# Pairs of tiles of one expert by Strassen's seven products, in a mixture-of-experts kernel whose bound is TensorE

## The chip, the cores and the metric

The kernel runs on one core of a Trainium2 chip. The metric is the device time of one execution in microseconds (us). All arithmetic that matters here is float32. The engines are called TensorE (PE in the profile, its weight loads PEld), VectorE (DVE), ScalarE (ACT), GpSimd (POOL) and SyncE (SP). SBUF and PSUM are the two on-chip memories that hold the program's tiles (matmuls write to PSUM), and the large arrays lie in DRAM. A transfer (DMA) *lands* when the profile shows it complete. The *granted clock* is the share of full speed that the profile gives for TensorE.

## The reference, cut to what matters

A causal linear attention (not touched by the change) makes 3072 tokens of 512 values. Each token then goes to one of eight experts, and its expert is two dense layers:

```python
h = np.maximum(x[b, s] @ w1[e], 0.0)      # 512 -> 1024
out[b, s] = p[e] * (h @ w2[e])            # 1024 -> 512
```

The expert `e` follows from the token's logits and a second gate, so how many tokens each expert gets is known only while the kernel runs. The kernel sorts the tokens by expert into tiles of up to 128 tokens (a half tile holds up to 64): a gather fetches a tile's rows from DRAM, and a scatter writes the result rows to their places.

## The kernel before

Most of the time after the attention goes into tiles, one after the other, in this order.

```python
def hidden(g, half):                      # layer 1 of tile g, half of the 1024 columns
    # ... (for half 0: a new buffer hts[g])
    ph = pg.tile([P, FT // 2, P], F32, name=f"ps{half}")
    for i in range(FT // 2):
        f = FT // 2 * half + i
        for d in range(DT):
            nc.tensor.matmul(ph[:, i], lhsT=w1t[g % 2][:, d, P * f:P * f + P], rhs=xtt[g % 2][:, d],
                             start=(d == 0), stop=(d == DT - 1))
    nc.scalar.activation(hts[g][:, FT // 2 * half:FT // 2 * half + FT // 2], ph, ACT.Relu)

def output(g):                            # layer 2
    ht = hts.pop(g)
    for f in range(FT):
        nc.tensor.matmul(pys[g % 2], lhsT=ht[:, f], rhs=w2t[g % 2][:, f], start=(f == 0), stop=(f == FT - 1))

def written(g):                           # times the chance, then the scatter
    i, j = at(g)
    y = act.tile([P, DM], F32, name="y")
    nc.vector.tensor_scalar(y, pys[g % 2], gate[i][:, j:j + 1], None, ALU.mult)
    nc.gpsimd.indirect_dma_start(out=out, out_offset=bass.IndirectOffsetOnAxis(ap=sidx[i][:, j:j + 1], axis=0),
                                 in_=y, in_offset=None, bounds_check=N - 1, oob_is_err=False)
# ... in an arm of the program, for each tile:
ahead(g + 2)                              # gather of the tile after the next, GpSimd
hidden(g, 0)
hidden(g, 1)
turned(g + 1)                             # four transposes of the next tile, copied to SBUF
output(g)
written(g)
weights(g + 2)                            # 4 MB of weights, if the expert changes
```

Counts that depend on the data (how many half tiles, how many extra tiles) are handled by branches into arms, one arm for each count.

## Time and profile before

| | before |
|---|---|
| time, median of the runs beside the changed kernel | 493.98 us (492.26 to 494.51, 4 runs) |
| span of the profiled run | 493.0 us |
| TensorE busy | 475.2 us, 96% |
| mean granted TensorE clock | 0.991 |
| VectorE / GpSimd busy | 127.3 / 106.8 us |

This is GpSimd's timeline in the same stretch of the kernel before (start us, duration us, then engine, line, operation, what is written and read; in brackets how long the engine sat idle before it, and what ended that):

```profile
341.17 1.00 POOL L659 DMA_INDIRECT out_dram<-y,sidx  x1 [5.29 <-DVE y L658]
347.96 1.04 POOL L621 DMA_INDIRECT xg<-x_dram,gidx  x1 [5.79 <-PE po L636]
355.62 1.01 POOL L659 DMA_INDIRECT out_dram<-y,sidx  x1 [6.62 <-DVE y L658]
```

GpSimd only starts gathers and scatters here. Scatters are 14.45 us apart, one for each tile, and each waits for its data. The list of GpSimd's waits (us in total, times, longest) has, among others, this:

```profile
POOL out_dram L659 <- DVE y L658: 179.3, 21, 13.9
...
POOL out_dram L829 <- DMA out_dram<-y,sidx: 13.2, 2, 6.6
```

A scatter that follows another scatter soon (L829 is a half tile's, issued right behind a full tile's) waits until the earlier one has landed, up to 6.6 us. Both write the tensor `out`, and the built program puts a wait for the first one's landing before the second. Between full tiles this wait is over long before the data is ready, so it can't be seen.

### The profile page before, as it was taken

The numbers are of one execution on the slowest core, as the hardware profiler recorded it, in microseconds if no ns is written. First come the engines' busy times: TensorE is split into PE (matmuls) and PEld (weight loads), VectorE is DVE, ScalarE is ACT, GpSimd is POOL, SyncE is SP. The second block draws the span as 40 slices with busy tenths as digits, with TensorE's granted clock in tenths as the row PEclk, the third lists the DMA queues.
The fourth block names the chain that finished last, engine by engine and source line by source line (L and its number), as shares of the span: only waits on it lengthen the run. The fifth ranks groups of instructions, "written<-read, shape, count | busy, mean of one in ns | idle before, by whom it ended". The sixth has DMA issues, their size and how long they took to land. (4 is left out here: it accounts for less than half of the span.)

```text
span 493.0 us, 10193 instructions
## 1 busy us (share of the span) xinstructions
PE 475.2 (96%) x4231; PEld 351.6 (71%) x4231; DVE 127.3 (26%) x315; ACT 84.7 (17%) x212; POOL 106.8 (22%) x118
## 2 busy tenths in 40 slices
PE   6999999989999999999999999999999999999992
PEld 5877788776777667658657856876667777666770
DVE  6645677652367301011010101101110110110000
ACT  2256656331110000000000001000000000000000
POOL 5575564300101300221011100201101101110000
PEclk9899999999999999999999999999999999999997
DMA  7999999996788999999999997699954980894000
GB/s 272 411 418 380 352 342 330 401 368 233 260 319 292 324 378 399 395 376 397 398 333 386 398 398 277 211 330 319 327 194 157 310 314 31 284 332 169 23 25 17
DMA packets 49850, 146.42 MB, mean 297 GB/s; under 512 B 3244, under 2 KB 3244, under 8 KB 46960
## 3 DMA queue, kind: packets, MB, share of 16 engines
q1 hardware_dynamic: 42096, 125.86, 69.9%
q0 software_dynamic: 4224, 13.37, 7.1%
q10 hardware_dynamic: 3456, 6.29, 3.4%
q8 instruction: 36, 0.59, 0.5%
q14 instruction: 38, 0.31, 0.2%
HBM read 153.90 MB, written 12.98 MB: 338 GB/s over the span
## 5 line engine op out<-in xcount | busy, mean ns | idle before, releaser
L646 PEld LDWEIGHTS ps<-xt,w 128*128 128x128 f32 x1536 | 175.0, 192 | 14.0 <-issue 12.9
L646 PE MATMUL ps<-xt,w 128*128 128x128 f32 x1536 | 177.1, 276 | 0.8 <-DVE xt L631 0.8
L653 PE MATMUL pk<-w,ht 128*128 128x512 f32 x384 | 168.8, 592 | 0.0
L653 PEld LDWEIGHTS pk<-w,ht 128*128 128x128 f32 x384 | 71.1, 190 | 80.4 <-issue 80.4
L648 ACT ACTIVATE ht<-ps 128x512 f32<-128x512 f32 x48 | 28.7, 598 | 314.7 <-PE ps L646 314.2
L659 POOL DMA_INDIRECT out_dram<-y,sidx x24 | 24.6, 1026 | 196.3 <-DVE y L658 179.3
L658 DVE TENSOR_SCALAR y<-pk,gate 128x512 f32<-128x512 f32 x24 | 18.0, 751 | 146.0 <-PE pk L653 140.6
L637 DVE COPY xt<-po 128x512 f32<-128x512 f32 x23 | 15.9, 691 | 143.2 <-PE po L636 143.1
L621 POOL DMA_INDIRECT xg<-x_dram,gidx x24 | 25.0, 1041 | 121.2 <-PE po L636 84.1
L189 DVE TENSOR_TENSOR sm<-ps,mask 128x512 f32<-128x512 f32 x46 | 29.6, 685 | 15.1 <-PE ps L185 15.0
L165 POOL TENSOR_TENSOR qd<-inp,lamq 128x512 f32<-128x512 f32 x20 | 25.6, 1282 | 23.3 <-PE po L212 8.8
L185 PE MATMUL ps<-inp 64*64 64x128 f32 x736 | 26.3, 282 | 2.0 <-DMA inp<-in_qkv_dram 2.0
L225 PE MATMUL po<-sm,inp 128*64 128x128 f32 x384 | 26.9, 284 | 0.3 <-DMA inp<-in_qkv_dram 0.3
L225 PEld LDWEIGHTS po<-sm,inp 128*64 128x64 f32 x384 | 21.1, 140 | 7.5 <-issue 6.6
L168 POOL TENSOR_TENSOR kd<-inp,rev 128x512 f32<-128x512 f32 x20 | 22.4, 1122 | 16.1 <-PE pk L234 7.6
L185 PEld LDWEIGHTS ps<-inp 64*64 64x64 f32 x736 | 20.6, 136 | 5.6 <-issue 4.6
L246 ACT COPY xn<-pk 128x512 f32<-128x512 f32 x24 | 14.1, 588 | 30.6 <-DMA x_dram<-xn 19.8
L216 ACT ACTIVATE kv<-kv,lamq 128x64 f32<-128x64 f32 x64 | 17.1, 337 | 9.8 <-PE po L212 6.4
L228 ACT COPY xc<-po 128x256 f32<-128x256 f32 x48 | 15.3, 371 | 14.2 <-PE po L225 14.0
L244 PE MATMUL pk<-ident,xc 128*128 128x128 f32 x96 | 15.7, 286 | 0.0
L234 PE MATMUL pk<-inp,kd 128*64 128x64 f32 x320 | 13.2, 222 | 1.2 <-issue 1.1
L636 PE MATMUL po<-ident,xg 128*128 128x128 f32 x92 | 13.8, 273 | 0.0
(182 smaller groups left out, 223.6 us busy)
## 6 DMA issues: line engine op xcount, KB each, us to landing
w<-in_w_dram SPq DMA_DIRECT2D x57, 2048.0 KB
inp<-in_qkv_dram SPq DMA_DIRECT2D x22, 1024.0 KB
x_dram<-xn ACTq DMA_DIRECT2D x24, 256.0 KB
inp<-in_qkv_dram SPq DMA_DIRECT2D x4, 512.0 KB
w<-in_w_dram SPq DMA_DIRECT2D x4, 512.0 KB
xg<-x_dram,gidx POOLq DMA_INDIRECT x24, 7.0
out_dram<-y,sidx POOLq DMA_INDIRECT x24, 6.9
xgh<-x_dram,gidx POOLq DMA_INDIRECT x3, 6.4
```

The costliest lines, as they stand in the source:

```text
L165: nc.gpsimd.tensor_tensor(qd, x[:, 0].rearrange("p (a i) -> p a i", i=P), lamq, ALU.mult)
L168: nc.gpsimd.tensor_tensor(kd.rearrange("p (h d) -> p h d", d=DH), x[:, 2].rearrange("p (h d) -> p h d", d=DH), rev.unsqueeze(2).broadcast_ ...
L185: nc.tensor.matmul(ps[u][js, a], lhsT=kt[rows, a, js], rhs=qt[rows, a], start=True, stop=True, skip_group_check=True)
L189: nc.vector.tensor_tensor(sm[:, u], ps[u], mask[:, u], ALU.mult)
L216: nc.scalar.mul(kv[:, a], kv[:, a], lamq[:, a, P - 1:P])
L225: nc.tensor.matmul(head(a, u), lhsT=vn[:, a, u], rhs=sm[:, u, a], start=(not c and a < 2), stop=True, skip_group_check=True)
L621: nc.gpsimd.indirect_dma_start(out=xg, out_offset=None, in_=x_dram[:n, :], in_offset=bass.IndirectOffsetOnAxis(ap=gidx[i][:, j:j + 1], axi ...
L646: nc.tensor.matmul(ph[:, i], lhsT=w1t[g % 2][:, d, P * f:P * f + P], rhs=xtt[g % 2][:, d], start=(d == 0), stop=(d == DT - 1))
L648: nc.scalar.activation(hts[g][:, FT // 2 * half:FT // 2 * half + FT // 2], ph, ACT.Relu)
L653: nc.tensor.matmul(pys[g % 2], lhsT=ht[:, f], rhs=w2t[g % 2][:, f], start=(f == 0), stop=(f == FT - 1))
L658: nc.vector.tensor_scalar(y, pys[g % 2], gate[i][:, j:j + 1], None, ALU.mult)
L659: nc.gpsimd.indirect_dma_start(out=out, out_offset=bass.IndirectOffsetOnAxis(ap=sidx[i][:, j:j + 1], axis=0), in_=y, in_offset=None, bound ...
```

## The change

The intent: two tiles of one expert form a pair, and each layer's product is cut into 2 x 2 blocks and computed by Strassen's seven block products in place of eight. TensorE does an eighth less for these tiles; VectorE and GpSimd make the block sums. What doesn't fit into pairs stays as full and half tiles. In the cut below `a1` and `b2` are blocks of the pair's weights `w1` and `w2`, `xs`, `s1`, `s2` and `hs` hold sums of blocks of x, of the weights and of the hidden values, and `product_1` and `product_2` are one block product of layer 1 and of layer 2. Calls of `hook`, which place the half tiles' work, are left out.

```diff
+    def sum_1(p, n):                       # block sums of w1, for layer 1 of pair p
+        x, y = ((a1(p, 0, 0), a1(p, 1, 1)), (a1(p, 1, 0), a1(p, 1, 1)), (a1(p, 0, 0), a1(p, 0, 1)))[n]
+        nc.vector.tensor_tensor(s1[:, n], x, y, ALU.add)
+        if n:
+            z = a1(p, 0, 0) if n == 1 else a1(p, 1, 1)
+            x = a1(p, 1, 0) if n == 1 else a1(p, 0, 1)
+            nc.gpsimd.tensor_tensor(x, x, z, ALU.subtract)     # in place
     # sum_2(p, n): the same for w2, L826 and L830 of the changed kernel
+    def pair(p, hooks={}, next=True, load=True, after=None):
+        if next:
+            pair_ahead(p + 1)                                  # two gathers
+        product_1(a, a1(p, 0, 0), xs[:, 1], True)
+        nc.scalar.copy(u, a)
+        product_1(c, a1(p, 1, 1), xs[:, 2], True)
+        nc.vector.tensor_tensor(u, u, c, ALU.add)
+        sum_2(p, 0)
+        product_1(b, s1[:, 0], xs[:, 0], True)
+        nc.scalar.copy(w, b)
+        sum_2(p, 1)
+        product_1(d, a1(p, 1, 0), xs[:, 3], True)
+        nc.gpsimd.tensor_tensor(w, w, u, ALU.add)              # L881
+        nc.vector.tensor_tensor(w, w, d, ALU.add)              # L882
+        sum_2(p, 2)
     # ... three more products of layer 1, ReLUs, sums of hidden blocks
+        product_2(x[:, :D2], h10, b2(p, 0, 1), True)           # needs GpSimd's difference L830
+        product_2(y[:, :D2], h01, b2(p, 1, 0), True)           # needs the other one
     # ... five more products of layer 2; among them sum_1(p + 1, 1), (p + 1, 2), (p + 1, 0)
+        nc.gpsimd.tensor_tensor(c11, c11, c00, ALU.add)        # L919
+        scatter(KA + 2 * p + 1, yt[:, 1])                      # after the sixth product
+        scatter(KA + 2 * p, yt[:, 0])                          # after the seventh
```

In the run's data there are eight pairs, three full tiles between the third and the fourth pair, and three half tiles within the first two pairs.

## The prediction

> **What bounds the kernel now.** I read the page first (busy shares and slices), then TensorE's timeline in a steady stretch, then the groups by shape, then the waits.
>
> ```profile
> PE 475.2 (96%) x4231; PEld 351.6 (71%) x4231; DVE 127.3 (26%) x315; ACT 84.7 (17%) x212; POOL 106.8 (22%) x118
> PE   6999999989999999999999999999999999999992
> ```
>
> TensorE is busy in every slice, while VectorE and GpSimd are nearly idle after the first third. That a busy TensorE really works back to back is seen in its timeline (start us, duration us):
>
> ```profile
> 339.94 7.31 PE L646 MATMUL ps<-xt,w 128*128 128x128 f32 x64
> 347.08 0.60 PE L636 MATMUL po<-ident,xg 128*128 128x128 f32 x4
> 347.52 7.03 PE L653 MATMUL pk<-w,ht 128*128 128x512 f32 x16
> 354.39 7.31 PE L646 MATMUL ps<-xt,w 128*128 128x128 f32 x64
> ```
>
> From start to start: layer 1 of a tile takes 7.14 us (64 issues of 111.6 ns; a float32 product is two issues), four transposes 0.44 us, layer 2 6.87 us (16 issues of 429.4 ns). A tile of 128 tokens is 14.45 us, without a gap at a wait or at the branches into arms, so two tiles are 28.9 us. A half tile adds 8.45 us (191.67 to 229.02 us holds two tiles and one half: 37.35 - 28.90). The list of waits has TensorE waiting 0.8 us in all for VectorE at layer 1: everything else waits for TensorE.
>
> **What the Trainium skill says.**
> 1. "TensorE: Matmul & The Clock Gate", section Back-to-back issue gap: N/2.4 + 2.5 ns per matmul. The trace agrees for float32 if its columns count double: 2 x 512/2.4 + 2.7 = 429.4. An issue of 256 columns, which the trace lacks at full width, I estimate so at 216 ns.
> 2. "SBUF — State Buffer", section Who interferes with whom: a VectorE instruction with two SBUF inputs and a GpSimd instruction that reads SBUF exclude each other, for the whole instruction. The trace agrees:
>
> ```profile
> 69.55 1.81 POOL L168 TENSOR_TENSOR kd<-inp,rev 128x512 f32<-128x512 f32 x1 [0.31 <-PE pk L234]
> 81.24 1.28 POOL L165 TENSOR_TENSOR qd<-inp,lamq 128x512 f32<-128x512 f32 x1 [1.49 <-issue]
> ```
>
> ```profile
> 69.26 1.19 DVE L413 TENSOR_TENSOR lane<-countb,place 128x1024 bf16<-128x1024 bf16 x1
> 81.84 0.79 DVE L445 TENSOR_TENSOR more<-incl,whole 128x96 f32<-128x96 f32 x1
> ```
>
> The VectorE sum of 96 elements, 0.26 us where alone (L349), takes 0.79 us and ends 0.11 us after the GpSimd product over which it lies; the GpSimd product, 1.04 us where alone, takes 1.81 us when it starts under a VectorE instruction. Only the fixed 0.15 us of the blocked one is hidden.
> 3. "VectorE: DVE Perf Modes", section on the TRN2 errata: a float32 tensor_tensor takes (N+151)/0.96 ns. L445 with 192 elements took 353 ns (357 by the formula), so 1024 elements are 1.22 us, 512 are 0.69, 256 are 0.42.
> 4. "GPSIMD Engine Reference", section Elementwise: 4497 ns for 2048 elements. With the trace's 1.28 us for 512 this makes 2.1 ns an element: my estimate for 1024 elements is 2.35 us.
>
> **The change part by part.** How many pairs there are follows from the data: I ran the reference's gate on its inputs. The experts get 410, 373, 371, 423, 434, 362, 354, 345 tokens. Five first tiles (one of each of experts 0 to 4) stay; the rest makes 8 pairs, 3 full tiles and 3 half tiles, the same 24 full and 3 half tiles as before (the page has 24 and 3 scatters).
>
> TensorE, removed: a pair takes seven products per layer in place of eight. Layer 1: 7 x 16 issues x 111.6 ns = 12.50 us (before 14.28). Layer 2: 7 x 8 issues x 216 ns = 12.11 us (before 13.74). With eight transposes (0.88) a pair is 25.5 us instead of 28.9: 3.4 us each, 27 us for eight. This is the ceiling of the gain.
>
> Added to VectorE, per pair: six weight sums of 1024 elements (7.3 us), four sums of x (1.95), five of hidden blocks (3.45), two final differences (0.85): 13.6 us with two SBUF inputs, and 4.7 us with one from PSUM. Added to GpSimd: four differences of 1024 elements (9.4), sums of 512 and 256 (1.28 + 0.74): 11.4 us, all reading SBUF. By item 2 these 13.6 and 11.4 us can't overlap: 25.0 us of one shared resource in a pair of 25.5 us. That decides the case, not the 18 us of VectorE.
>
> Where it reaches TensorE: the order of the built program (which I read engine by engine) puts the sums for the next pair's layer 1 into the end of the pair. From the end of the third product of layer 2 to the first product of the next pair runs this chain: drain and handover 0.23, ScalarE copy of 256 columns 0.37 (L228), handover 0.2, GpSimd sum 0.74, GpSimd difference 2.35 with VectorE's second sum shut out, that sum 1.07, handover 0.2, GpSimd difference 2.35 with VectorE's third sum shut out, that sum 1.07, VectorE's final difference 0.36, sum of x 0.36, restart 0.18: 9.48 us. TensorE has four products and four transposes there, 4 x 1.73 + 0.44 = 7.36 us. It waits 2.1 us. So a pair is 27.6 us, not 25.5.
>
> The whole, along TensorE. (a) Routing: VectorE's work on tables grows (tables of five columns, 480 in place of 288 elements twice, six more small instructions of 0.2 us, one more list of owners): 3.4 us by the rows of L486 to L528. Its slack is seen here:
>
> ```profile
> 151.38 0.67 DVE L637 COPY xt<-po 128x512 f32<-128x512 f32 x1
> ```
>
> TensorE takes this copy at 153.91; now it ends 1.6 us after that. The slot matmuls have 190 columns, not 150: 0.3 us. Tile 4 starts at 169.96 + 1.9 = 171.9. (b) Tile 4 with both transposes of pair 0 14.95 us, then TensorE waits 1.5 us for the copy and the first sum of x, because nothing lies between: pair 0 starts at 188.4. (c) Work from there: 8 x 24.61 + 14 sets of transposes 6.2 + 3 full tiles 43.4 + 3 halves 25.3 = 271.8 us. (d) Waits: pairs 0 and 1 have the halves' matmuls over them and wait 0.95 each; before the full tiles the x copy stands behind all sums on VectorE (4.0) and the second gather (7.0 us to landing) comes 1.1 late; pairs 3 to 6 wait 2.14 each; the last pair makes no sums. Sum 15.6. TensorE ends at 475.8, against 484.0. (e) The tail is as before, 9.1 us; time over span 1.5 us. 475.8 + 9.1 + 1.5 = 486.4 us.
>
> **The rivals.** *No exclusion on the new sums.* If VectorE and GpSimd ran side by side the waits of pairs would vanish; by the same sum about 473 us. The two overlaps above speak against it. *GpSimd slower.* Its differences are in place and strided, which no row shows; every 0.1 us on 2.35 adds 0.2 us to each of five waits and, above 2.6, further waits inside the pair: 490 us or more. *Weight loads as bound.* A pair loads 4 MB in 27.6 us, 150 GB/s, where the page shows slices of 398 GB/s; next weights are issued a pair ahead; and a pair loads its expert once. Hidden. *Many more waits on TensorE.* Each product now starts with one; the timeline shows no gap at the satisfied waits of before. *Issues of 256 columns slower*, 229 ns as in the half tiles' rows (3.67 us for 16 concurrent pairs): 0.7 us a pair, of which part falls into the wait: about 490.
>
> **Range and chances.** The ceiling is 27 us minus about 3.4 of entry costs, 472; what takes it away is five waits whose size is a difference of two long sums, so some 5 us either way, and the unforeseen mostly costs. The hooks look tuned, which speaks for smaller waits; I put the middle at 485.5, just above the 2% line of 484.6. Range 476 to 492; faster 0.43, same 0.53, slower 0.04.
>
> **What would show it.** Right: layer 1 products at 1.79 us and layer 2 at 1.73 in the timeline of TensorE; pair starts 27 to 28 us apart in the last arm; TensorE waiting about 2 us once per pair, for VectorE's sum of x; VectorE's rows of 1024 elements with a mean well over 1.22 us, and GpSimd's differences near 2.4. Wrong: gaps inside the pair rather than at its start, pair starts at 25.5 us (no exclusion), TensorE waiting for weights or for gathers, or a layer 2 issue that isn't near 216 ns.

## More of the kernel before

`PE`, `DVE` and `SP` take their work in program order; the order of ScalarE and GpSimd is chosen by the scheduler.

## The result, and the profile after

The changed kernel takes 532.44 us (median of 4 runs, 531.79 to 538.17), the kernel before 493.98 us on the same chip. The ratio of the fast runs is 1.0812, with a 95% interval of 1.0744 to 1.088: slower. (A ratio is the mean time of one kernel's fast runs over the mean of the other's from the same rounds, so it is not quite the ratio of the medians quoted beside it.) The profiled run took 538.17 us, its span is 536.5 us, and the mean granted clock is 0.953 in place of 0.991.

These lines of the page answer to those shown of before (busy time and share, then TensorE's busy tenths and its granted clock in 40 slices of 13.4 us):

```profile
PE 468.6 (87%) x4295; PEld 384.0 (72%) x4295; DVE 277.0 (52%) x499; ACT 124.3 (23%) x292; POOL 208.2 (39%) x166
...
PE   6999998999999997999993974999798689898891
...
PEclk9899998999999998999998787999989799999997
```

There are holes in the second half, and the clock goes down in the slices at the holes and behind them. One pair on TensorE's timeline, the fifth:

```profile
404.78 2.02 PE L841 MATMUL ps<-xs,w 128*128 128x128 f32 x16 [1.61 <-issue]
406.63 1.95 PE L841 MATMUL po<-xs,w 128*128 128x128 f32 x16
...
415.57 1.95 PE L841 MATMUL ps<-xp,s 128*128 128x128 f32 x16
422.45 6.50 PE L846 MATMUL pk<-w,h 128*128 128x256 f32 x16 [4.94 <-POOL w L830]
428.79 0.60 PE L651 MATMUL po<-ident,xg 128*128 128x128 f32 x4
```

The products of layer 1 start 1.79 us apart, as predicted (five of them from 406.63 to 415.57). Before the pair TensorE waits 1.6 us, not far from the 2.1 predicted. Then comes something that the prediction didn't have: a gap of 4.94 us at the first product of layer 2, for GpSimd's difference. And the two products behind the gap take 6.34 us from start to start (428.79 - 422.45) where 16 issues of 216 ns would be 3.46. GpSimd in the same pair:

```profile
404.62 1.29 POOL L669 DMA_INDIRECT out_dram<-y,sidx  x1 [1.69 <-DVE y L937]
412.45 1.90 POOL L669 DMA_INDIRECT out_dram<-y,sidx  x1 [6.54 <-DMA out_dram<-y,sidx]
416.45 1.04 POOL L636 DMA_INDIRECT xg<-x_dram,gidx  x1 [2.10 <-PE po L841]
417.79 1.02 POOL L636 DMA_INDIRECT xg<-x_dram,gidx  x1 [0.30 <-PE ps L841]
418.84 1.27 POOL L881 TENSOR_TENSOR part<-part 128x512 f32<-128x512 f32 x1
420.05 2.35 POOL L830 TENSOR_TENSOR w<-w 128x1024 f32<-128x1024 f32 x1
```

Read it from below. TensorE's gap ends when the first L830 has ended (422.40). L830 stands behind L881, L881 behind two gathers, and the gathers behind the second scatter. The second scatter has stood still for 6.54 us until the first scatter had landed, although its data (VectorE's L945) was ready at 406.28. Two gathers behind one another don't wait like that (416.45 and 417.79): in the built program a scatter waits for the landing of the scatter before it, and a gather doesn't wait for the gather before it. GpSimd takes its work in order, so all sums behind this scatter are late. GpSimd isn't overloaded: it has nothing to do in that time.

The longest of TensorE's waits in the whole run, and two of GpSimd's:

```profile
PE pk L846 <- POOL w L830: 25.2, 8, 9.1
PE po L651 <- DMA xg<-x_dram,gidx: 7.7, 1, 7.7
PE ps L841 <- DVE xs L833: 7.2, 5, 1.8
```

```profile
POOL out_dram L669 <- DMA out_dram<-y,sidx: 46.7, 8, 7.6
POOL xg L636 <- DMA out_dram<-y,sidx: 17.1, 3, 8.0
```

How long the second scatter stands still depends on the pair. In six of the eight pairs it waits 6.5 to 7.6 us; the core's DMA engines are 78 to 90% busy between the two scatters there, with weights on their way. In the last two pairs no weights are left to load, the DMA engines are 17 and 19% busy, and the wait is 2.95 us at the end and 2.5 us here:

```profile
504.02 0.99 POOL L669 DMA_INDIRECT out_dram<-y,sidx  x1 [2.50 <-DMA out_dram<-y,sidx]
```

Behind this shorter wait, in the last pair, which issues no gathers either, TensorE doesn't wait for a difference. So it is probably the traffic of the weights that makes the landing slow. No run tests that.

The second line of GpSimd's list is gathers before which the profile sees a wait for a landing. What the third pair's scatters do to the full tiles behind it is seen here, on TensorE and on GpSimd:

```profile
315.88 8.72 PE L659 MATMUL ps<-xt,w 128*128 128x128 f32 x64 [3.43 <-issue]
332.31 1.09 PE L651 MATMUL po<-ident,xg 128*128 128x128 f32 x4 [7.70 <-DMA xg<-x_dram,gidx]
333.19 8.32 PE L665 MATMUL pk<-w,h 128*128 128x512 f32 x16
```

```profile
313.52 1.28 POOL L669 DMA_INDIRECT out_dram<-y,sidx  x1 [1.70 <-DVE y L937]
321.42 1.00 POOL L669 DMA_INDIRECT out_dram<-y,sidx  x1 [6.62 <-DMA out_dram<-y,sidx]
325.57 1.04 POOL L636 DMA_INDIRECT xg<-x_dram,gidx  x1 [3.15 <-DMA out_dram<-y,sidx]
```

The gather of the second full tile stands behind the third pair's two scatters. It is issued 12 us after the first of them, and TensorE waits 7.7 us for its rows. The prediction had 1.1 us there.

So my theory after the traces (A): what makes the change slow is GpSimd's queue. The second scatter of each pair waits in it for the landing of the first, and sums and gathers that TensorE needs soon stand behind. The gaps that this makes in TensorE's work then cost more than their length, since the clock goes down. The rivals: (B) the mutual exclusion of VectorE and GpSimd, my prediction's own cause, is larger than I took it for, and GpSimd's lateness is its consequence; (C) the order in which the scheduler put GpSimd's work; (D) VectorE is too full.

An account along TensorE helps to weigh them. From the first pair's start to TensorE's end I add up the rows of its timeline at full-rate durations (an issue of 128 columns 111.7 ns, of 256 columns 216 ns, of 512 columns 429.4 ns) and call this work; I add up the idle times in brackets; what is left over is time in which matmuls ran slower than at full rate.

| us | predicted | changed kernel |
|---|---|---|
| first pair starts | 188.4 | 190.7 |
| work from there | 271.8 | 271.2 |
| idle from there | 15.6 | 45.1 |
| below full rate | 0 | 18.1 |
| TensorE ends | 475.8 | 525.1 |

The saving is there: the kernel before takes 299.5 us from the same point on (184.5 to 484.0), without a gap, so TensorE has 28.3 us less to do. That is buried under 63 us of gaps and slow stretches.

### The profile page after: what moved, and what is told of

Same layout as the page of the kernel before. It is cut to its first block, busy times and chain, and to the rows that moved or that the text cites. A ratio compares the mean times of both kernels' runs of the same rounds, so it can differ in the third digit from the quotient of the medians.

```text
span 536.5 us, 10737 instructions
## 1 busy us (share of the span) xinstructions
PE 468.6 (87%) x4295; PEld 384.0 (72%) x4295; DVE 277.0 (52%) x499; ACT 124.3 (23%) x292; POOL 208.2 (39%) x166
## 4 chain that ended last, share of the span: by engine, by line
PE 41%; DMA 24%; issue 14%; DVE 14%; POOL 5%; another core or an unknown queue 0%; SPq 0%; POOLq 0%; ACT 0%; DVEq 0%
DMA out_dram<-y,sidx 22%; PE pk L846 6%; DVE s L818 5%; PE ps L185 4%; PE po L225 4%; PE ps L841 4%; PE pk L665 4%; PE ps L659 3%; PE pk L244 2%; PE pr L986 2%; PE pr L967 2%; PE po L841 2%; DMA inp<-in_qkv_dram 2%; PE pk L234 2%; POOL w L830 2%
## 5 line engine op out<-in xcount | busy, mean ns | idle before, releaser
L659 PEld LDWEIGHTS ps<-xt,w 128*128 128x128 f32 x512 | 59.4, 196 | 8.9 <-issue 5.8
L659 PE MATMUL ps<-xt,w 128*128 128x128 f32 x512 | 60.6, 280 | 5.4 <-issue 3.4
L846 PE MATMUL pk<-w,h 128*128 128x256 f32 x128 | 40.7, 479 | 25.2 <-POOL w L830 25.2
L665 PE MATMUL pk<-w,h 128*128 128x512 f32 x128 | 57.5, 603 | 0.0
L818 DVE TENSOR_TENSOR s<-w 128x1024 f32<-128x1024 f32 x24 | 53.6, 2239 | 0.0
L846 PEld LDWEIGHTS pk<-w,h 128*128 128x128 f32 x128 | 29.3, 240 | 33.6 <-POOL w L830 28.9
L822 POOL TENSOR_TENSOR w<-w 128x1024 f32<-128x1024 f32 x16 | 39.5, 2474 | 18.3 <-DVE s L818 11.1
L665 PEld LDWEIGHTS pk<-w,h 128*128 128x128 f32 x128 | 24.3, 195 | 27.6 <-issue 27.6
L846 PE MATMUL pk<-s,hsum 128*128 128x256 f32 x192 | 43.6, 380 | 0.0
L830 POOL TENSOR_TENSOR w<-w 128x1024 f32<-128x1024 f32 x16 | 37.7, 2356 | 8.6 <-DVE s L826 8.6
L841 PE MATMUL ps<-xs,w 128*128 128x128 f32 x256 | 32.0, 278 | 10.0 <-DVE xs L833 7.2
L841 PEld LDWEIGHTS ps<-xs,w 128*128 128x128 f32 x256 | 29.9, 192 | 13.4 <-DVE xs L833 9.2
L846 PEld LDWEIGHTS pk<-s,hsum 128*128 128x128 f32 x192 | 35.6, 190 | 5.2 <-issue 0.8
L826 DVE TENSOR_TENSOR s<-w 128x1024 f32<-128x1024 f32 x24 | 39.3, 1665 | 0.0
L165 POOL TENSOR_TENSOR qd<-inp,lamq 128x512 f32<-128x512 f32 x20 | 25.6, 1281 | 25.9 <-PE po L212 12.4
L225 PE MATMUL po<-sm,inp 128*64 128x128 f32 x384 | 27.6, 285 | 2.8 <-issue 2.4
```

The costliest lines, as they stand in the source:

```text
L225: nc.tensor.matmul(head(a, u), lhsT=vn[:, a, u], rhs=sm[:, u, a], start=(not c and a < 2), stop=True, skip_group_check=True)
L659: nc.tensor.matmul(ph[:, j], lhsT=w1t[w][:, d, P * f:P * f + P], rhs=xtt[i][:, d], start=(d == 0), stop=(d == DT - 1))
L665: nc.tensor.matmul(pys[i], lhsT=hq[f // 4, i][:, f % 4], rhs=w2t[w][:, f], start=(f == 0), stop=(f == FT - 1))
L818: nc.vector.tensor_tensor(s1[:, n], x, y, ALU.add)
L822: nc.gpsimd.tensor_tensor(x, x, z, ALU.subtract)
L826: nc.vector.tensor_tensor(s2[:, n], x, y, ALU.add)
```

## The experiments

Eight kernels ran, all correct. Kernels sent together share the runs of the kernel before (medians 493.98 to 496.76 us in the four sets of runs, that of the changed kernel included). A ninth idea, one scatter for both tiles of a pair, did not build, since the indirect DMA takes one index per partition here.

### e1_late_scatter and e2_program_order: the second scatter moved, and its control

```diff
 # e1: the second scatter of pair p waits for a place in pair p + 1
-        scatter(KA + 2 * p, yt[:, 0])
+        kept.append(lambda: scatter(KA + 2 * p, y0))    # y0: yt[:, 0], or an unused tile for odd pairs
 # ... in the next pair, behind both differences L830 in GpSimd's order:
+        if kept:
+            kept.pop()()
 # e1 and e2: GpSimd in program order, with w += u ahead of the difference
-    with tc.manual_schedule(engines={PE, DVE, SP}):
+    with tc.manual_schedule(engines={PE, DVE, SP, mybir.EngineType.Pool}):
```

> GpSimd in program order; a pair's second scatter is issued in the middle of the next pair, behind that pair's differences for layer 2 (odd pairs keep the result in an unused buffer). All sums stay on GpSimd and VectorE, so their exclusion is as before. Theory A (GpSimd's queue stands still until the first scatter has landed, 6.5 to 7.6 us, and the differences for layer 2 stand behind it): the 25.2 us of waits at the first product of layer 2 fall below 6 us and the granted clock rises from 0.953 towards 0.98; time 497 to 510 us. Rival B (VectorE and GpSimd shut each other out, and that alone makes the pair long): the same sums collide, time 525 us or more.

> Control for the one before: GpSimd in program order too, but the two scatters stand one behind the other as in the changed kernel. Theory A: the wait for the landing is still there, time 525 to 542 us. If the order alone were what helps (rival C: the scheduler's order of GpSimd), this would be as fast as the kernel with the late scatter.

Measured: the late scatter 519.88 us (517.61 to 525.31), the control 543.64 us (542.97 to 544.51), the kernel before 494.89 us; ratios 1.054 (1.0469 to 1.061) and 1.0979 (1.0938 to 1.1019). The two differ in nothing but the place of the second scatter and its buffer, and they are 23.8 us apart. In the control the wait for the difference is as in the changed kernel, and a little longer:

```profile
PE pk L846 <- POOL w L830: 28.1, 8, 10.4
```

With the late scatter the wait for the difference falls from 28.1 to 13.5 us, and the clock rises from 0.947 to 0.981. That is theory A's direction and the end of B as the main cause, since not one sum was moved between engines; C falls too, since program order alone costs 11 us. But the time is 10 us above my range, and 13.5 us of the wait are left where I expected less than 6. The timeline tells where: in the pairs that follow a branch, and in the first. There the gathers, which program order puts at the start of the pair, stand ahead of the sums and wait themselves; in the fourth pair, which follows a branch, the first gather came 8.7 us after the last full tile's scatter, 7.75 of them standing still (the profile puts the wait down to a matmul). In the last three pairs no difference stands behind a wait for a landing, and this is how GpSimd then looks:

```profile
432.96 2.35 POOL L831 TENSOR_TENSOR w<-w 128x1024 f32<-128x1024 f32 x1
436.54 2.36 POOL L831 TENSOR_TENSOR w<-w 128x1024 f32<-128x1024 f32 x1 [1.23 <-DVE s L827]
439.06 1.03 POOL L669 DMA_INDIRECT out_dram<-y,sidx  x1 [0.16 <-issue]
```

The first difference ends at 435.31, before TensorE needs it at 437.58, and there is no gap inside the pair. These pairs start at 424.97, 452.33 and 479.70: 27.4 us each, where I had predicted 27.6, with a wait of 1.6 us at the start of each for VectorE's sums of x. So the collisions of VectorE and GpSimd, which B makes the whole loss, cost about what I said.

### e3_differences_on_vector and e4_all_on_vector: the sums off GpSimd

```diff
 # e3: in sum_1 and sum_2
-            nc.gpsimd.tensor_tensor(x, x, z, ALU.subtract)
+            nc.vector.tensor_tensor(x, x, z, ALU.subtract)
 # e4: these too
-        nc.gpsimd.tensor_tensor(w, w, u, ALU.add)
+        nc.vector.tensor_tensor(w, w, u, ALU.add)
-        nc.gpsimd.tensor_tensor(c11, c11, c00, ALU.add)
+        nc.vector.tensor_tensor(c11, c11, c00, ALU.add)
```

> The four weight differences of a pair go from GpSimd to VectorE; the two small sums and the scatters stay on GpSimd. Theory A: VectorE now waits for GpSimd's small sum, which still stands behind the second scatter, so the gap moves from the first product of layer 2 to a later one that needs a sum of hidden blocks, about 4 to 6 us a pair: time 505 to 530 us. Rival B: 25.0 us of shared resource become some 18 us of VectorE, and the whole loss vanishes: time 485 us or less.

> All six GpSimd sums of a pair go to VectorE (24.3 us of its work in a pair of 25.5 us by the durations in the trace); GpSimd only issues gathers and scatters. Theory A and rival B both expect the pair near 25.5 to 27 us and no wait of TensorE for GpSimd; what stays is the wait for the second full tile's gather (7.7 us): time 480 to 495 us. If VectorE is too full (rival D), pairs of 28 us and 500 us or more.

Measured: e3 528.78 us (524.2 to 531.4), ratio 1.068 (1.06 to 1.076); e4 502.29 us (501.44 to 504.1), ratio 1.0142 (1.0102 to 1.0183). In e3 the four long differences are gone from GpSimd, and with them nearly all of the exclusion, and the time hardly moves. One small sum of 1.27 us (L881) is still behind the scatter; VectorE waits for it, ScalarE's ReLU (L894, behind another ReLU) for VectorE, and TensorE for the ReLU:

```profile
410.80 1.89 PE L846 MATMUL pk<-w,h 128*128 128x256 f32 x8
419.20 3.78 PE L846 MATMUL pk<-w,h 128*128 128x256 f32 x8 [6.51 <-ACT h L894]
```

There are six such gaps, 26.0 us in all, against 25.2 us of the changed kernel: the same loss, at the second product of layer 2 in place of the first. This is the plainest answer to B: take the exclusion away and leave the queue, and the loss stays. In e4 nothing that TensorE needs is behind a scatter, except gathers. Its pairs are 26.6 us apart (413.28, 439.86, 466.43), and VectorE, now with all sums, keeps up, which speaks against D. The time is 7 us above the upper end of my range. I had counted one wait for a gather, of 7.7 us; there were four, 12.4 us in all, 9.1 of them before the second full tile, and I had left out the time below full rate, here some 7 us.

### e5_vector_gathers_first and e6_gpsimd_gathers_first: the gathers ahead of the scatters too

```diff
 # both: pair p issues the gathers of pair p + 2 right behind its own transposes, ahead of its scatters
-        if next:
-            pair_ahead(p + 1)
+            pair_turned(0)
+            ahead(KA + 2 * p + 4, 0)
 # ...
+            pair_turned(1)
+            ahead(KA + 2 * p + 5, 1)
 # the full tiles' first two gathers likewise, in the second and third pair;
 # the first full tile is copied by ScalarE, one product earlier
 # e5 alone: e4's sums on VectorE, one weight sum earlier, e1's second buffer but no late scatter
 # e6 alone: e1's late scatter, and the sums on GpSimd as in the change
```

> All sums on VectorE as in the fourth run, GpSimd in program order with every gather issued a pair earlier and ahead of that pair's scatters, the first full tile gathered to the half tiles' buffer and copied by ScalarE, odd pairs' results of their first tile in another buffer, one weight sum moved ahead. Theory A: the waits for gathers (12.4 us of the fourth run, 9.1 of them before the second full tile), the wait before the first full tile (1.6) and the 0.7 us waits before the last product but one go, and with them the half-rate stretches after them: 502.3 - 12.4 - 1.6 - 3.7 - about 3 = 482 us, range 478 to 488, clock 0.985 or more. If those waits are only moved to another place in GpSimd's queue: 495 us or more.

> The first run (second scatter late, sums divided between VectorE and GpSimd as in the change) with the gathers a pair earlier as well: the change without its queue waits, so that the exclusion of VectorE and GpSimd is all that is left of the losses. My prediction's sum for this case: a pair of 27.6 us (27.4 in the undisturbed pairs of the first run) against 26.6 in the fourth: 484 to 493 us. If the waits at the first product of layer 2 are due to anything else than the queue, such as GpSimd's load (rival B), they stay at 10 us or more: 500 us or more.

Measured: e6 498.1 us (496.17 to 499.78), ratio 1.0008 (0.9958 to 1.0059), the same as before. e5 489.25 us (483.28 to 492.82), ratio of its fast runs 0.9756 (0.969 to 0.982), which leaves open whether it is 2% faster (unclear); three of its six runs count as slow, being over 1.5% above its fastest, and the profiled run is one of them. Its fast runs took 485.2 us on average, within the range; the median is 1 us above it. The kernel before took 496.76 us beside them.

e6 is the change with its sums where they were and the queue put in order (and the first full tile copied by ScalarE): 34 us faster than the changed kernel, a ratio to the kernel before of 1.0008 in place of 1.0812. What is left of the 25.2 us:

```profile
PE pk L848 <- POOL w L832: 5.2, 4, 1.6
```

It missed my range by 5 us. By the account along TensorE it has 271.2 us of work, 18.7 us idle behind the first pair's start and 5.5 us below full rate. Of the idle time 8.9 us are the waits for sums of x (predicted 10.5), 4.4 us are at the full tiles (predicted 5.1), and 5.2 us are four waits for a layer 2 difference that I didn't have, in the first pair and in those behind a branch.

The undisturbed pairs give the price of sharing the sums between the two engines: 27.4 us in e6 (406.03, 433.39, 460.76), against 26.6 us in e4, where VectorE makes them in the same order, and 25.8 us in e5 (401.72, 427.51, 453.30), where one of them comes earlier. The profile of e5 is of a slow run; e8, which has the same order and was profiled in a fast one, shows the same 25.8 us. With everything on VectorE a pair is thus at the 25.5 us that I had counted for TensorE's work, plus 0.3.

In e5 one gather was still behind a scatter, that of the third full tile: 3.5 us of waiting, and the layer behind it took 9.25 us in place of 7.03.

### e7_gaps_in_before: what a gap costs by itself

```diff
 # the kernel before, in hidden(g, half)
+        if half and g >= 6 and g % 2 == 0:
+            for _ in range((4, 8, 12, 16)[(g - 6) // 2 % 4]):
+                nc.scalar.activation(hts[g][:, FT // 2:], hts[g][:, FT // 2:], ACT.Relu)
```

> The kernel before with TensorE made to wait inside nine tiles: ScalarE repeats its ReLU in place 4, 8, 12 or 16 times on the second half of the hidden block, so layer 2 stops in its middle for some 0.9, 3.1, 5.3 or 7.5 us (an estimate from 0.55 us a repeat). The gaps add up to about 34 us. If a gap costs its own length only: 529 us, granted clock 0.99. If the granted clock falls after a long gap as it seems to in the changed kernel (1.5 to 2 us more after gaps above some 4 us): about 536 us and a clock of 0.96 or less, with matmuls at half rate after the long gaps and not after the short ones.

Measured: 538.3 us (2 runs, 536.92 and 539.67), 496.76 before, clock 0.964. Six gaps came about (four repeats fit into the time that there is, so they make none). Four of them, and the half product behind each:

```profile
255.18 3.70 PE L656 MATMUL pk<-w,ht 128*128 128x512 f32 x8 [2.01 <-ACT ht L651]
...
292.90 6.42 PE L656 MATMUL pk<-w,ht 128*128 128x512 f32 x8 [4.31 <-ACT ht L651]
```

```profile
403.33 5.40 PE L656 MATMUL pk<-w,ht 128*128 128x512 f32 x8 [2.10 <-ACT ht L651]
...
438.94 5.09 PE L656 MATMUL pk<-w,ht 128*128 128x512 f32 x8 [4.75 <-ACT ht L651]
```

Eight issues of 512 columns take 3.44 us at full rate. From each start to the next row's, they took 3.63, 6.25, 5.23 and 4.92 us here, and 6.50 and 6.43 us behind two gaps of 7.39 us. So the gaps are 28.0 us long in all, and the stretches behind them lose another 12.3 us: together 40.3, against 41.5 us by which the time went up. A gap of 2 us lost 0.2 us in one place and 1.8 in another; those of 4.3 us and more lost 1.5 to 3.1 us. I expected that a short gap is free, and one wasn't. TensorE's own work is as before here, so the slow stretch behind a gap is not Strassen's doing.

### e8_third_gather_first: the last gather put right

```diff
 # e5, the third pair
-        pair(2, ..., then=[lambda: None, lambda: ahead(G1 + 1, 1)])
+        pair(2, ..., then=[lambda: ahead(G1 + 2, 0), lambda: ahead(G1 + 1, 1)])
 # and the same gather taken out of the arms of the full tiles
```

> The fifth run with the third full tile's gather too moved ahead of the second pair's scatters (it stood behind the first full tile's scatter; TensorE waited 3.5 us for it and then ran some 2 us at half rate). If the account by gaps and half-rate stretches holds, that run's time falls by 5 to 6 us: about 483 us, range 478 to 487, a ratio to the kernel before of 0.965 to 0.975. If something else paces that stretch: no change.

The second pair of this text is `pair(2)`, counted from 0; it is called the third pair elsewhere here.

Measured: 481.3 us (479.97 to 481.95, 5 runs), the kernel before 495.24 us, ratio 0.9716 (0.9691 to 0.9741): faster than both kernels. The first lines of its page:

```profile
PE 450.7 (94%) x4295; PEld 371.4 (77%) x4295; DVE 287.8 (60%) x546; ACT 123.5 (26%) x293; POOL 115.8 (24%) x118
...
PE   6899998999999999999999999999998999999990
...
PEclk9999999999999999999999999999999999999997
```

The holes are gone, the clock is 0.994. By the account: work 271.2, idle behind the first pair's start 4.1, below full rate 2.9 us. The span is 13.1 us shorter than before (479.9 against 493.0), while TensorE's work is 28.3 us less. The other 15 us: the first pair starts at 190.0 where the same point lies at 184.5 before, the 4.1 and the 2.9 us, and 2.6 us at the end, where the last pair's second scatter waits for the first.

## Why the prediction was wrong, point by point

The prediction was 485.5 us, with 492 as its upper end, so a small gain or none; the change took 532.44 us, a clear loss.

- **TensorE's work: right.** Products of layer 1 at 1.79 us, an issue of 256 columns at 216 ns (24 of them in 5.18 us), 271.2 us from the first pair on against 271.8. (The prediction's point 1 agrees with the trace at 512 columns only: with doubled columns it gives 109.4 ns for 128, where the trace has 111.6. Its sum used the trace's value.) The satisfied waits at each product cost nothing, and no weight load was waited for.
- **The exclusion of VectorE and GpSimd, and the chain at the pair's start: right.** VectorE's sums of 1024 elements took 2.24 us on average in the layer 1 groups, and 1.22 us in e8, where GpSimd does no sums. An overlap in the changed kernel, in the form of those in the prediction:

```profile
435.93 2.36 POOL L822 TENSOR_TENSOR w<-w 128x1024 f32<-128x1024 f32 x1 [1.22 <-DVE s L818]
436.04 3.33 DVE L818 TENSOR_TENSOR s<-w 128x1024 f32<-128x1024 f32 x1
```

  The wait at the start of a pair is 1.6 us (predicted 2.1), an undisturbed pair 27.4 us (27.6), GpSimd's differences 2.36 to 2.47 us (2.35). e4 puts its price at 0.8 us a pair, e5, with one sum earlier, at 1.6 us; both are below what the queue cost.
- **"Added to GpSimd": the step that failed.** I counted what GpSimd computes, 11.4 us a pair, and didn't follow its queue. What it holds in order is also two gathers and two scatters, and I took the scatters to be as free as they were before. Before, a scatter came every 14.45 us; a pair has two ready within 2 us, and the second waits for the landing of the first, 6.5 to 7.6 us in all pairs but the last two. The prediction looks for the chain only from the end of the third product of layer 2 to the next pair; the scatters come at the end of that chain, and what stands behind them is the beginning of the next pair. So the waits of 25.2 us at the first products of layer 2 are missing from its list (d). That the queue is the cause is shown by e1 against e2 (only the scatter moved, 23.8 us), by e3 (sums moved, queue left, nothing gained) and by e6 (sums left, queue put right, 34 us gained).
- **"The second gather comes 1.1 late": wrong by the same cause.** I timed the gather from its own landing time and not from its place behind two scatters. It was 7.7 us, and 9.1 in e4. With the gathers ahead of the scatters (e8) there is no wait at the full tiles.
- **The clock: not in the prediction at all.** I counted a gap at its length. The 18.1 us that TensorE lost below full rate are a third of the 51.8 us by which the profiled run (538.2 us) missed the sum (486.4). e7 shows that gaps alone do this.
- **The routing and the entry (a, b): nearly right.** The wait for the copy of x by VectorE is 1.14 us, predicted 1.6, and the first pair starts at 190.7, predicted 188.4. This is the line on TensorE's timeline:

```profile
157.39 2.83 PE L659 MATMUL ps<-xt,w 128*128 128x128 f32 x23 [1.14 <-DVE xt L652]
```

- **The tail (e): off by 2.3 us.** From TensorE's end to the span's end it is 11.4 us, not 9.1. The last pair's second scatter is issued 2.5 us after its data was ready (VectorE's L945 ends at 526.26, the scatter starts at 528.75), again for the first one's landing.
- **The rivals.** "GpSimd slower" comes closest in what it forecasts, further waits inside the pair, but its reason isn't what happened: the differences took 2.36 us. "TensorE waiting for gathers" and "gaps inside the pair" stand among the signs that would show the prediction wrong. The chances didn't follow from that: 0.04 for slower says that I took the sum for complete. "The hooks look tuned" was an argument from the code's looks, which no run tests by itself.
- **The sum.** Against the 486.4 us that it comes to, the profiled run has 2.3 us at the first pair's start, -0.6 of work, 29.5 of idle time, 18.1 below full rate and 2.3 at the end: 51.6 of 51.8 us. With the queue right and the rest as it was, e6 still took 498.1 us, so even without the failed step the value was some 12 us too low: the entry, the four waits in the first pair and behind branches, the tail, and 5.5 us below full rate (1.7 of them behind the gap of 3.3 us at a full tile, the rest spread in small pieces).

What stays open: why a gap of 2 us leaves the clock alone in one place and not in another (in e3, e4, e6 and e8 single gaps of 1.9 us and less were followed by 0.3 us of loss at most, and one of 2.02 us in e4 by 1.7); whether the weights' traffic makes the landings slow; and why the pairs behind a branch wait for a difference in e1 and e6, which I only saw and didn't test.

## What to carry to other kernels

Before work is given to an engine that is "nearly idle", follow its queue in order and list what it waits for there, satisfied waits too: a wait that is hidden while two scatters are 14 us apart becomes a wait of 7 us when they are 2 us apart, and all that stands behind it inherits it. Put gathers ahead of scatters, and keep work with a deadline off a queue that waits for landings. And where the bound is TensorE, count a gap at its length plus up to 3 us: a hole of 5 us a pair is more than the 3.4 us that the seven products save.

## What the Trainium skill lacked or had wrong

- "DMA: Bandwidth & Descriptors", section "Anatomy of one DMA — SWDGE (gpsimd) path", fits a DMA of GpSimd by 2.0 us and the bytes at 436 GB/s, which is 2.6 us for a scatter of 256 KB (128 rows of 2 KB; an estimate from that fit). The scatters of the changed kernel landed 6.8 us after their issue at the median (2.6 at the least, 8.3 at the most), and gathers of the same size after 6.6 us. The page's figure was met where little else was moving: the last four scatters, with no weights on their way, landed after 2.7 to 3.2 us. The fit has no term for other traffic. It is this landing time that the second scatter stood still for.
- No page tells that two indirect writes into one tensor, built by this framework, wait for one another's landing: 46.7 us of waiting of GpSimd in 8 times in the changed kernel.
- "TensorE: Matmul & The Clock Gate", section "What's actually happening", has the clock at half after at least one idle window of about 3.4 us, and back at full after at least one busy window of that length. Here a gap of 2.1 us was followed by 1.8 us of loss, another of 2.0 us by 0.2 us, and gaps of 4.3 to 7.4 us by 1.5 to 3.1 us (e7). The eight issues behind the gaps of 7.4 us took 6.4 to 6.5 us in place of 3.44, so nearly all of them ran at half rate, which is almost two such windows. The shortest gap that cost something is shorter than the text makes one expect, and the price of a gap was up to 3.1 us, where one window at half rate would make 1.7 us (an estimate from the page's 3.4 us).
- "SBUF — State Buffer", section "Who interferes with whom", has the exclusion that the prediction rests on, and the runs agree. It gives no durations for two elementwise sums that meet: a difference of 1024 elements costs GpSimd 2.36 us and VectorE 1.23 us (e4), and shuts the other out for that time, so a pair got 0.8 us shorter when all such sums went to VectorE (27.4 us in e1, 26.6 in e4).
